# A new lead-in, logits in groups of eighty and a new order, in a kernel of windowed attention and a GELU layer

One core of a Trainium2 chip. The metric is the device time of one execution in microseconds (us), median over executions; a lower one is better.

## The reference

The input is normalised once and goes through two branches, whose results are added to it.

```python
xn = layernorm(x)                          # x: 2048 x 640, bf16
qkv = xn @ wqkv                            # 32 heads of 20
# query s sees keys s, s-2, ..., s-14 (8 of them); keys before the start are masked
attn = softmax(mask(q . k[s - 2w]) * 20**-0.5)
A = (sum_w attn[w] * v[s - 2w]) @ wo
B = gelu_tanh(xn @ w1 + b1) @ w2 + b2      # 640 -> 1536 -> 640
return x + A + B
```

## The kernel before

It works in four chunks of 512 positions (0 to 3), each of four blocks of 128. A planner in the kernel lists the pieces of work (name, engine, estimated duration, what they need), simulates the engines, and issues the pieces in the order in which they started in that simulation. Each engine gets its instructions in this order; in the traces below they wait for one another in it (a root whose input was ready at 4.87 us started at 7.15, behind a sum that waited for its data). `PE` is TensorE, `VE` VectorE, `SE` ScalarE, `DQ` the SyncE queue.

```python
# loads of the lead-in (cut)
nc.sync.dma_start(x_sb[:, 0, :], x_nb[:, 0, :])
nc.scalar.dma_start(x_sb[:, 1, :], x_nb[:, 1, :])
for s in range(3):                                     # q's, k's, v's weights, 800 KB each
    nc.sync.dma_start(wqkv[s][:], wqkv_v[:, :, s * D : (s + 1) * D])
    if s == 1:
        nc.sync.dma_start(x_sb[:, 2:BPC, :], x_nb[:, 2:BPC, :])
...
# 44 warm-up matmuls on zeros, then the plan
for _ in range(WARM):
    nc.tensor.matmul(idle[:, 0, :], lhsT=zeros[:], rhs=zeros[:], start=True, stop=True)
for t in make_plan(fns).run():
    t["fn"]()
```

For each block of chunk 0 VectorE takes the statistics (`st`), ScalarE the root (`rs`), VectorE the reciprocal and the normalised block (`rc`, `xn`), TensorE the transposes (`tp`), ScalarE copies them out of PSUM (`tc`), and TensorE projects block by block (`gj`, 128 columns a matmul, into the PSUM tile `gps`).

```python
def do_tp(n, bl, a, b):
    xn = tiles["xn", n, bl]
    tp = get(("tp", n, bl), lambda: psA.tile([P, 2 * CH], BF16, tag="acc", name="tp"))
    for t in range(a, b):
        nc.tensor.transpose(tp[:, t * P : (t + 1) * P], xn[:, t * P : (t + 1) * P], ident[:])
...
# logits: VectorE's eight products of q and shifted k fill four buffers "prod" (the whole pool);
# TensorE sums them by head: 20 matmuls for each buffer
group = 2 if n else 4
if wp % group == group - 1:
    wps = range(wp - group + 1, wp + 1)
    ...
    pl.add(f"lg{n}{wp}", PE, 0.16 + 0.52 * group, n - 1000, need, f("lg", n, wps), every + [L], slack=0.8)
...
def do_xs(n):                  # attention weights spread over each head's channels, half of it
    expand(nc.scalar, n, (2, 3))
def do_xd(n):                  # the other half
    expand(nc.sync, n, (0, 1))
```

ScalarE also empties the four PSUM accumulators of later chunks' projections (`pc`), applies GELU, and copies the output blocks.

## Time and profile before

| | before |
|---|---|
| time, median (range) | 215.03 us (215.01 to 215.15, 3 runs) |
| span of the profiled run | 212.4 us |
| TensorE, VectorE, ScalarE busy | 97%, 82%, 52% of the span |
| first useful matmul, last matmul (starts) | 7.03 us, 209.42 us |

The span goes from the first to the last instruction in the trace. The lines behind this table are shown and read in the prediction.

### The profile page before, as it was taken

To read this page: it belongs to the slowest core of one execution; us is meant where nothing else is said; L and a number is where in the kernel's file an instruction comes from. 1 tells how busy PE (TensorE), PEld (TensorE's weight loads), DVE (VectorE), ACT (ScalarE), POOL (GpSimd) and SP (SyncE) were. 2 spreads that over 40 slices of the span, in tenths; PEclk is the share of its full clock that TensorE was granted. 3 is DMA by queue.
4 is the path that set the end of the run, shared out by engine and by line. 5 is a ranking of instruction groups with operands and counts; after the bars stand their busy time and mean duration, and the time that the engine had idled before them with its cause. 6 is when DMAs were issued, how large, how long until landed. Compare 5 with 4: busy or idle time off the path is not lost.

```text
span 212.4 us, 3961 instructions
## 1 busy us (share of the span) xinstructions
PE 206.9 (97%) x1670; PEld 121.7 (57%) x1693; DVE 174.4 (82%) x178; ACT 109.5 (52%) x193; POOL 19.7 (9%) x37
## 2 busy tenths in 40 slices
PE   8999999999999999999999999999999999999994
PEld 8799845655545555555555555455555455555552
DVE  3579999759999997599996999999999999972001
ACT  3568997798574654931353883503752511341120
POOL 2000000000020024101100010101110011101130
PEclk9999999999999999999999999999999999999999
DMA  6999528916829199993120027202114611122214
GB/s 216 365 362 376 93 50 275 322 24 132 206 64 163 37 287 196 197 195 89 15 30 0 0 31 200 31 3 31 14 21 48 180 19 22 27 29 31 34 16 76
DMA packets 23465, 23.95 MB, mean 113 GB/s; under 512 B 9112, under 2 KB 20632, under 8 KB 23448
## 3 DMA queue, kind: packets, MB, share of 16 engines
q1 hardware_dynamic: 17864, 16.49, 28.3%
q0 software_dynamic: 4144, 4.92, 17.2%
q10 hardware_dynamic: 1440, 2.29, 3.9%
q8 instruction: 13, 0.21, 0.4%
q14 instruction: 4, 0.03, 0.1%
HBM read 10.00 MB, written 7.54 MB: 83 GB/s over the span
## 4 chain that ended last, share of the span: by engine, by line
PE 97%; issue 1%; DVE 0%; ACT 0%
PE lo L684 27%; PE hps L653 24%; PE pps L484 23%; PE gps L501 8%; PE hi L686 8%; PE L L557 4%; PE idle L725 2%; PE tp L437 1%; ACT xnT L441 0%; DVE osb L714 0%; DVE zeros L361 0%
## 5 line engine op out<-in xcount | busy, mean ns | idle before, releaser
L653 PE MATMUL hps<-xnT,w_sb 128*128 128x512 bf16 x235 | 54.1, 379 | 0.3
L684 PE MATMUL lo<-w_sb,hT 128*128 128x512 bf16 x183 | 51.8, 379 | 0.0
L631 DVE TENSOR_TENSOR pv<-vT,ax 128x2560 bf16<-128x2560 bf16 x32 | 45.9, 1484 | 1.7 <-PE L L557 1.7
L535 DVE TENSOR_TENSOR prod<-qT,kT 128x2560 bf16<-128x2560 bf16 x32 | 45.4, 1484 | 0.0
L686 PE MATMUL hi<-w_sb,hT 128*128 128x128 bf16 x192 | 40.3, 219 | 0.6 <-issue 0.2
L664 ACT ACTIVATE hT<-hps,b1T 128x512 bf16<-128x512 f32 x48 | 31.6, 687 | 17.0 <-PE hps L653 13.3
L653 PEld LDWEIGHTS <-w_sb 128*128 128x128 bf16 x240 | 23.0, 98 | 26.7
L640 DVE TENSOR_TENSOR pv<-pv 128x5120 bf16<-128x5120 bf16 x12 | 33.9, 2825 | 0.4
L684 PEld LDWEIGHTS <-hT 128*128 128x128 bf16 x192 | 18.7, 98 | 22.8 <-issue 0.6
L691 ACT CAST osb<-lo 128x512 bf16<-128x512 f32 x15 | 8.8, 585 | 44.0 <-issue 28.0
L697 POOL DMA_DIRECT2D out_dram<-osb x15 | 12.9, 863 | 110.5 <-ACT osb L692 110.5
L684 PE MATMUL lo<-wo,oT 128*128 128x512 bf16 x79 | 23.0, 379 | 0.0
L686 PEld LDWEIGHTS <-hT 128*128 128x128 bf16 x192 | 18.4, 98 | 1.5
L398 DVE BATCH_NORM_STATS2 stats<-x_sb 128x6 f32<-128x320 bf16 x32 | 14.0, 469 | 5.1 <-DMA x_sb<-in_A_x_dram 5.1
L484 PE MATMUL pps<-xnT,wq_sb 128*128 128x512 bf16 x71 | 16.9, 380 | 0.2
L484 PE MATMUL pps<-xnT,wv_sb 128*128 128x512 bf16 x73 | 16.9, 379 | 0.1
L686 PE MATMUL hi<-wo,oT 128*128 128x128 bf16 x80 | 16.9, 219 | 0.1
L484 PE MATMUL pps<-xnT,wk_sb 128*128 128x512 bf16 x73 | 16.8, 379 | 0.1
L705 DVE TENSOR_TENSOR osb<-lo,x_sb 128x512 bf16<-128x512 f32 x1 | 0.7, 692 | 16.1 <-PE lo L684 16.1
L520 ACT CAST qT<-pps 128x512 bf16<-128x512 f32 x15 | 8.8, 585 | 9.2 <-PE pps L484 9.2
L684 PEld LDWEIGHTS <-oT 128*128 128x128 bf16 x80 | 7.8, 98 | 9.4
L484 PEld LDWEIGHTS <-wk_sb 128*128 128x128 bf16 x75 | 8.7, 118 | 7.3 <-issue 0.2
(62 smaller groups left out, 205.9 us busy)
## 6 DMA issues: line engine op xcount, KB each, us to landing
w_sb<-in_B_w_dram SPq DMA_DIRECT2D x2, 1920.0 KB, 9.2
out_dram<-osb POOLq DMA_DIRECT2D x15, 160.0 KB, 3.4
ax<-attn SPq DMA_DIRECT2D x8, 256.0 KB, 5.4
ax<-attn ACTq DMA_DIRECT2D x8, 256.0 KB, 5.6
out_dram<-x_sb SPq DMA_DIRECT2D x3, 640.0 KB, 4.3
out_dram<-b2bc POOLq DMA_DIRECT2D x3, 640.0 KB, 8.2
x_sb<-in_A_x_dram SPq DMA_DIRECT2D x1, 1280.0 KB, 13.3
wq_sb<-in_A_wqkv_dram SPq DMA_DIRECT2D x1, 800.0 KB, 4.8
```

Of the source, the lines that this page charges most:

```text
L398: nc.vector.bn_stats(stats[:, i, :], x_sb[:, b, i * (D // 2) : (i + 1) * (D // 2)])
L484: nc.tensor.matmul(ps[:], lhsT=wqkv_p[which][:, ti, to, :], rhs=xnT[:, ti, :], start=(ti == 0), stop=(ti == KT - 1),)
L501: nc.tensor.matmul(ps[:, i, :], lhsT=wqkv_p[which][:, ti, to, :], rhs=tiles["xnT", 0][:, ti, cs], start=(ti == 0 and (i == 0 or b == KT an ...
L520: nc.scalar.copy(dest[:, to, off : off + CH], tiles["pps", n, which, to][:])
L535: nc.vector.tensor_tensor(out=prod[:, i, :, :], in0=qkv_tile(n, 0)[:], in1=qkv_tile(n, 1)[:, :, off : off + CH], op=ALU.mult,)
L631: nc.vector.tensor_tensor(out=pv[:, i, :, :].rearrange("p t (j c) -> p t j c", j=BPC), in0=qkv_tile(n, 2)[:, :, off : off + CH].rearrange( ...
L640: nc.vector.tensor_tensor(out=ta[:], in0=ta[:], in1=tb[:], op=ALU.add)
L653: nc.tensor.matmul(ps[:], lhsT=w1_sb[:, ti, ft * P : (ft + 1) * P], rhs=tiles["xnT", n][:, ti, :], start=(ti == 0), stop=(ti == KT - 1),)
L664: nc.scalar.activation(hT[:], tiles["hps", n, ft][:], ACT.Gelu_apprx_tanh, bias=b1T[:, ft : ft + 1], scale=1.0)
L684: nc.tensor.matmul(lo[:], lhsT=lhs, rhs=rhs[:, 0:CH], start=first, stop=last)
L686: nc.tensor.matmul(hi[:, 0 : D - CH], lhsT=lhs, rhs=rhs[:, CH:D], start=first, stop=last)
L697: nc.gpsimd.dma_start(rows, tiles["osb", n, bl][:], accum_op=ALU.add)
```

## The change

Its intent, as read from the diff: to start useful work earlier by having q's weights on the way first, to take block 1's statistics on an engine that is idle at that time (a sum, then a sum of squares on ScalarE), to copy block 0's and 1's transposes on two engines at once, to project later blocks in pairs (256 columns a matmul), to spend less on groups of logits, and to bring w1 earlier so that TensorE always has something to do. The planner gets new landing times and ranks. The diff, cut to its core:

```diff
+    for b in range(2):
+        nc.scalar.dma_start(x_sb[:, b, :], x_nb[:, b, :])
+    load_w(0)
+    load_x(2, BPC)
+    load_w(1)
+    load_w(2)
     ...
-            land = (4.0, 4.0, 9.6, 9.6)[bl] if n == 0 else (0.0, 13.3, 17.1, 17.1)[n]
+            land = (3.1, 3.6, 6.6, 6.6)[bl] if n == 0 else (0.0, 12.9, 21.8, 21.8)[n]
+            if n == 0 and bl == 1:
+                pl.add("sm", SE, 0.72, -99, [], f("sum1"), after=land)
+                pl.add("nm", SE, 0.22, -99, ["sm"], f("neg1"))
+                pl.add("me", VE, 0.12, -98, ["sm"], f("mean1"))
+                pl.add("sq", SE, 0.93, -99, ["nm"], f("sq1"))
+                pl.add("rs01", SE, 0.3, -99, ["sq"], f("sqrt", 0, 1, 2), table="sqrt")
+                pl.add("rc01", VE, 0.16, -99, ["rs01", "me"], f("rstd", 0, 1, 2))
+                continue
     ...
+                for u, a, b, eng, own in (("a", 0, 2, VE, "lo"), ("b", 2, KT, SE, "hi")):   # block 0: a PSUM tile each
     ...
-            group = 2 if n else 4
+        need = [f"qk{n}{x}{i}" for x in range(W // 2) for i in range(2)]
+        for wp in range(W // 2):          # all four buffers' logits follow one another
+            us, slack = (0.5, 0.0) if wp else (0.74, 0.8)
+            need = [pl.add(f"lg{n}{wp}", PE, us, n - 1000, need, f("lg", n, wp), [("prod", "qk", n, wp), L], slack=slack)]
-        pl.add(f"xs{n}", SE, 1.2, n - 1000, [f"at{n}"], f("xs", n), [at, ax])
+        pl.add(f"xs{n}", SE, 1.6, n - 1000, [f"at{n}"], f("xs", n), [at, ax])
     ...
+            nc.tensor.matmul(idle[:, 0, :], lhsT=ones, rhs=ones, start=True, stop=True)
```

Also in it: the maximum is subtracted in place in PSUM, w1 comes in two halves ahead of chunks 2 and 3, and the planner knows GpSimd's output writes as a queue.

## The prediction

> **What bounds the kernel now.** I read the page's busy shares and its chain first, to see which engine sets the end, then the list of what TensorE waits for, then the timeline of the lead-in, and last the timelines around one group of logits and around the last output of VectorE.
>
> ```profile
> PE 206.9 (97%) x1670; PEld 121.7 (57%) x1693; DVE 174.4 (82%) x178; ACT 109.5 (52%) x193; POOL 19.7 (9%) x37
> ...
> PE 97%; issue 1%; DVE 0%; ACT 0%
> ```
>
> TensorE is busy 97% of the span and the chain that ended last is TensorE for 97% of it. No other engine is on it for as much as a per cent. The waits of TensorE, summed over the whole span, are three:
>
> ```profile
> PE idle L725 <- DVE zeros L361: 1.0, 1, 1.0
> PE gps L501 <- ACT xnT L441: 0.5, 1, 0.5
> PE hi L686 <- issue: 0.2, 1, 0.2
> ```
>
> So there is no large wait to remove. What can go is time before the first useful matmul, and time per matmul. The lead-in, in the timeline (start, duration, engine, operation):
>
> ```profile
> 0.99 4.87 PE L725 MATMUL idle<-zeros 128*128 128x128 bf16 x44 [0.99 <-DVE zeros L361]
> ...
> 3.71 0.89 DVE L398 BATCH_NORM_STATS2 stats<-x_sb 128x6 f32<-128x320 bf16 x2 [2.77 <-DMA x_sb<-in_A_x_dram]
> ...
> 4.87 0.30 ACT L404 ACTIVATE std<-mv,eps_t 128x1 f32<-128x1 f32 x1 [2.18 <-DVE mv L400]
> 5.20 0.16 DVE L408 RECIPROCAL rstd<-std 128x1 f32<-128x1 f32 x1
> 5.40 0.63 DVE L424 TENSOR_SCALAR xn<-x_sb,mv,rstd 128x256 bf16<-128x256 bf16 x2
> ...
> 5.80 0.77 PE L437 MATMUL tp<-ident,xn 128*128 128x128 bf16 x5
> ...
> 6.61 0.75 ACT L441 COPY xnT<-tp 128x256 bf16<-128x256 bf16 x2 [1.44 <-PE tp L437]
> 7.03 1.28 PE L501 MATMUL gps<-xnT,wq_sb 128*128 128x128 bf16 x20 [0.46 <-ACT xnT L441]
> ```
>
> The reader is to see that useful work starts at 7.03 us and that its chain is block 0 of x: landing at 3.71, statistics, root, reciprocal, normalise, transpose, copy. The copy starts at 6.61 only after all five transposes, though its first part needs two. The last matmul starts at 209.42 (the closing five `hi` start at 209.20, 56 ns apart), so 202.4 us lie between the first and the last useful matmul and 3.0 us after it.
>
> A group of forty logits, and a group of eighty (chunk 0):
>
> ```profile
> 54.48 1.03 PE L484 MATMUL pps<-xnT,wv_sb 128*128 128x512 bf16 x4
> ...
> 55.44 1.27 PE L557 MATMUL L<-prod,head_of 128*32 128x256 bf16 x40
> ...
> 56.65 1.06 PE L484 MATMUL pps<-xnT,wv_sb 128*128 128x512 bf16 x3
> ```
>
> ```profile
> 36.83 2.37 PE L557 MATMUL L<-prod,head_of 128*32 128x256 bf16 x80
> 39.13 1.06 PE L484 MATMUL pps<-xnT,wq_sb 128*128 128x512 bf16 x3
> ```
>
> Forty take 55.44 to 56.65 = 1.21 us, eighty take 2.30 us: 27 ns each and 0.12 us per group. Before a group, four matmuls of 216 ns from 54.48 should end at 55.34, so about 0.09 us is lost on entering, and about 0.03 on leaving. One group's fixed price is thus about 0.24 us.
>
> [...] the row of 20 above gives (1.28 - 0.22)/19 = 56 ns, the row of 4 gives (1.03 - 0.38)/3 = 217. No row of before has N = 256 with full weights[...]. [...] The 44 warm-up matmuls are 0.107 us apart ((4.87 - 0.29)/43) and the first useful ones 0.056, so here the change fell between about 6.3 and 7.0 us[...]. [...] the trace has 0.93 for the two-pointer normalisation. [...] the page's GB/s row shows 362 to 376 in the first slices, so loads in the lead-in share a full pipe and only their order can be chosen.
>
> **The change part by part.**
> 1. *Start of useful work.* Block 0 now leaves from the ScalarE queue (where block 1 took 3.1 us from its issue at 0.75, against 2.9 for block 0 on the other), so it lands no earlier, about 3.7; q's weights leave first on the other queue, 0.46 earlier than now, so with 4.8 us to landing about 5.5, before they are wanted. Then 3.71 + 0.89 + 0.04 + 0.21 = 4.85, root 0.30 and reciprocal 0.16 with gaps to 5.37, first two slices normalised by 5.67, two transposes with their drain by 6.1, a 256-column copy of 0.36 now on VectorE and in its own PSUM tile by 6.45. First useful matmul about 6.5: **0.5 us** saved, nearly all of it from the copy no longer waiting for the other three transposes. The warm-up needs no VectorE memset and starts 0.2 earlier, ending at about 5.5; it doesn't limit.
> 2. *Projections of chunk 0.* Now 300 matmuls of N = 128: 300 x 0.056 = 16.8 us. After: 50 x 0.056 + 125 x 0.109 = 2.8 + 13.6 = 16.4. **0.4 us**, all of it on the path, since TensorE runs without gaps there. The two breaks for transposes (0.15 at 8.3 us, smaller later) may lose **0.1** more.
> 3. *Logits.* Chunks 1 to 3 go from six groups to three: 3 x 0.24 = **0.7 us** of TensorE.
> 4. *Block 1's statistics on ScalarE.* About 0.72 + 0.22 + 0.9 + 0.3 us of ScalarE, beside other work; VectorE loses 1.1 us. Not on the path, unless the first sum (block 1's landing, about 3.9 to 4.1, + 0.72 = 4.6 to 4.8) delays block 0's root at 4.87. That is tight, up to 0.2 us.
> 5. *In-place subtraction in PSUM, earlier w1, added DMA ordering in the plan.* They move no TensorE work. Earlier w1 only gives TensorE something else to do from some 16 us on; there is hardly a hole there to fill.
> The 737 matmuls of N = 512, the 272 of N = 128 in the outputs, and the 3.0 us after the last remain.
>
> Sum: start 6.5; work 202.4 - 0.4 - 0.1 - 0.7 = 201.2; end 3.0; span 210.7. For new small holes I add 0.3: 211.0. The measured time lies 215.03 - 212.4 = 2.6 above the span, so **213.6 us**, 0.7% less.
>
> **The rivals.**
> *VectorE takes the place.* A group of eighty holds all four product buffers until it is done, so VectorE can start no product of the earlier chunk for some 3 us in each of three chunks, where now half the buffers come back early. VectorE is nearly full from 23 us to 193:
>
> ```profile
> 131.11 11.30 DVE L535 TENSOR_TENSOR prod<-qT,kT 128x2560 bf16<-128x2560 bf16 x8
> 142.33 4.29 DVE L631 TENSOR_TENSOR pv<-vT,ax 128x2560 bf16<-128x2560 bf16 x3
> 146.53 1.22 DVE L570 TENSOR_REDUCE m<-L 128x128 f32<-128x1024 f32 x1
> ...
> 191.21 1.49 DVE L646 TENSOR_TENSOR oT<-pv 128x2560 bf16<-128x2560 bf16 x1 [1.58 <-PE hi L686]
> ```
>
> Here the three products at 142.33 run while the second half of the logits is computed; after the change they can't. Its last oT is done at 192.7 and first read at 195.89, and it waited 1.58 us for its buffer: some 4 to 5 us of slack. Against up to 9 us lost stand the new order, which can put later statistics (8 blocks, about 1 us each) into these gaps, and an earlier start of the first products by about 1 us. If VectorE comes out late by more than the slack, TensorE has only a few output blocks to do without oT: 1 to 4 us lost, a time of 214.5 to 217.
> *A long start.* If the clock is released a microsecond later than the first useful matmul, or block 0's root waits for ScalarE, part 1 gives back up to 0.5: 214.1.
> *No gain in part 1.* If block 0 shares the pipe with q's weights and lands at 4.2 instead of 3.7, the same: 214.1.
> *More than expected.* If q's weights and block 0 both come early (3.2 and 5.2), the start is 6.0 and the time 213.0. A gain over 2% would need 4.3 us, and the matmuls that remain leave no room for it.
>
> **Range and chances.** The sum is known to some 0.4 us on the fast side. On the slow side the open thing is the holes of the new order: none to two or three microseconds. Range 212.6 to 215.4. Faster by over 2%: 1%. Within 2%: 96%. Slower by over 2% needs over 4 us of new holes: 3%.
>
> **What would show it.** Right: first useful matmul at 6.2 to 6.7 us in the timeline; first copy of block 0 by VectorE directly behind two transposes; 256-column matmuls 0.109 apart; four groups of eighty in the chain; TensorE waits after the start below 0.5 us in sum; last `hi` matmul about 3.0 before the end. Wrong: TensorE waiting for VectorE or ScalarE in the list of waits, above all output matmuls on oT near the end; VectorE's last oT later than some 195 us; TensorE's busy time not lower by about 1 us; a start at or after 7.0.

## The result

| | before | after |
|---|---|---|
| time, median (range) | 215.06 us (215.01 to 215.15, 4 runs) | 220.33 us (219.17 to 220.58, 4 runs) |
| ratio, 95% interval | | 1.0234, 1.0209 to 1.0259 |
| span of the profiled run | 212.4 | 218.2 |
| first useful matmul, last matmul (starts) | 7.03, 209.42 | 8.84, 214.79 |

The change made the kernel slower by 2.3%. The mean granted clock of a run counts the time before the first entry of its clock record as full: the profiled run of the changed kernel lists 1.000, although TensorE is at half clock until 13.4 us (below). Two of its other three runs list 0.984, which is what 6.8 us at half clock after an earlier release would give (6.8/2/218 = 0.016). Ratios here are the mean time of one kernel's fast runs over that of the other's of the same rounds, so not quite the ratio of the medians quoted.

The page of the changed kernel, its busy shares and its chain:

```profile
PE 209.6 (96%) x1568; PEld 124.0 (57%) x1568; DVE 173.9 (80%) x177; ACT 108.2 (50%) x189; POOL 19.7 (9%) x37
...
PE 76%; DVE 16%; DMA 2%; ACTq 2%; ACT 1%; issue 1%
```

TensorE is still busy for nearly all of it, and its busy time is longer, although it has less to do: at half clock the matmuls take longer (fifteen in the lead-in below are 0.105 us apart, against 0.056 at full clock). The chain is no longer TensorE's alone. It begins with a DMA of x and ScalarE's queue. The waits of TensorE, in sum, number and longest:

```profile
PE tp L498 <- DVE xn L483: 2.4, 1, 2.4
PE pps L542 <- ACT vT L601: 1.8, 1, 1.8
PE idle L805 <- PEq L822: 0.8, 1, 0.8
PE pps L542 <- ACT kT L601: 0.3, 1, 0.3
```

The first is new, and stands before the first transpose. The lead-in in the timeline:

```profile
0.75 0.92 ACTq L384 DMA_DIRECT2D x_sb<-in_A_x_dram  x2
...
0.78 4.85 PE L805 MATMUL idle<-const-bfloat16-1.0 128*128 128x128 bf16 x44 [0.78 <-PEq L822]
...
4.66 0.21 DVE L444 BATCH_NORM_AGGREGATE mv<-stats 128x2 f32<-128x12 f32 x1
...
6.42 0.74 ACT L450 ACTIVATE xn<-x_sb 128x640 bf16<-128x640 bf16 x1 [3.22 <-DMA x_sb<-in_A_x_dram]
...
7.15 0.28 ACT L463 ACTIVATE std<-mv,eps_t 128x1 f32<-128x1 f32 x1
...
8.06 0.79 PE L498 MATMUL tp<-ident,xn 128*128 128x128 bf16 x5 [2.43 <-DVE xn L483]
...
8.49 0.29 DVE L503 COPY xnT<-tp 128x256 bf16<-128x256 bf16 x1 [0.20 <-PE tp L498]
...
8.84 1.76 PE L555 MATMUL gps<-xnT,wq_sb 128*128 128x128 bf16 x15
```

Block 0's statistics are done at 4.87. Its root starts at 7.15, because block 1's sum stands before it on ScalarE and waits until 6.42 for block 1. In the trace's DMA packets, ScalarE's queue moves block 0's share until about 3.3 us, nothing from there to 5.1, and block 1's share from 5.1 to 5.9; between the two SyncE's queue moves q's weights at 190 KB per half microsecond. TensorE stands from the end of its warm-up at 5.6 until 8.06, and then works at half clock: fifteen matmuls take (1.76 - 0.29)/14 = 0.105 us each. The trace's clock record has the release at 13.4 us, against 6.4 in the kernel before.

Later, the second wait of the list (timeline of 118 to 130 us):

```profile
117.35 7.09 DVE L710 TENSOR_TENSOR pv<-vT,ax 128x2560 bf16<-128x2560 bf16 x5
...
121.40 4.48 PE L542 MATMUL pps<-xnT,wv_sb 128*128 128x512 bf16 x20
...
124.47 2.38 ACTq L694 DMA_DIRECT2D ax<-attn  x2
...
126.89 0.25 ACT L608 COPY vT<-vT 128x70 bf16<-128x70 bf16 x1 [4.55 <-issue]
127.05 2.53 ACT L601 CAST vT<-pps 128x512 bf16<-128x512 f32 x5
...
127.68 1.24 PE L542 MATMUL pps<-xnT,wv_sb 128*128 128x512 bf16 x5 [1.80 <-ACT vT L601]
```

TensorE fills four accumulators with v's projections (20 matmuls) by 125.7. ScalarE can't empty them: the next thing in its order is to issue two transfers of attention weights, which wait until VectorE has read the tile of the chunk before (124.44), and then take 2.38 us to issue, where the plan counts 1.6.

The difference in span of 5.80 us, by the starts of the matmuls in the two traces:

| | before | after | difference |
|---|---|---|---|
| first useful matmul | 7.03 | 8.84 | +1.81 |
| matmuls and transposes at half clock after it (extra time) | 0 | 2.15 | +2.15 |
| the holes at 85.8, 125.5 and 175.3 us | 0 | 0.49 + 1.97 + 0.20 | +2.66 |
| all other time between first and last matmul | 202.39 | 201.14 | -1.25 |
| from the last matmul's start to the end | 2.99 | 3.42 | +0.43 |

The second row counts the 43 steps from 8.84 to the release at 13.4: they took 4.54 us, against 43 x 0.0557 = 2.39 at full clock.

### The profile page after: what moved, and what is told of

Read it like the earlier page. It is cut to its first block, busy times and chain, and to the rows that moved or that the text cites.

```text
span 218.2 us, 3727 instructions
## 1 busy us (share of the span) xinstructions
PE 209.6 (96%) x1568; PEld 124.0 (57%) x1568; DVE 173.9 (80%) x177; ACT 108.2 (50%) x189; POOL 19.7 (9%) x37
## 3 DMA queue, kind: packets, MB, share of 16 engines
q10 hardware_dynamic: 1584, 2.46, 4.4%
HBM read 10.00 MB, written 7.54 MB: 80 GB/s over the span
## 4 chain that ended last, share of the span: by engine, by line
PE 76%; DVE 16%; DMA 2%; ACTq 2%; ACT 1%; issue 1%
PE lo L763 22%; PE hps L732 22%; PE pps L542 15%; DVE pv L710 10%; PE gps L586 6%; PE hi L765 6%; PE L L637 3%; DMA x_sb<-in_A_x_dram 2%; PE gps L555 2%; ACTq L694 2%; DVE L L656 1%; DVE attn L684 1%; DVE m L650 1%; DVE rs L679 1%; PE tp L498 1%; DVE sums L674 1%
## 5 line engine op out<-in xcount | busy, mean ns | idle before, releaser
L763 PE MATMUL lo<-w_sb,hT 128*128 128x512 bf16 x192 | 53.4, 379 | 0.0
L442 DVE BATCH_NORM_STATS2 stats<-x_sb 128x6 f32<-128x320 bf16 x30 | 12.8, 466 | 3.7 <-DMA x_sb<-in_A_x_dram 3.7
L523 POOL DMA_DIRECT2D out_dram<-b2bc x4 | 5.3, 1322 | 102.6 <-DMA out_dram<-x_sb 102.4
L542 PEld LDWEIGHTS <-wv_sb 128*128 128x128 bf16 x75 | 8.7, 117 | 9.8 <-issue 2.7
```

The costliest lines, as they stand in the source:

```text
L442: nc.vector.bn_stats(stats[:, i, :], x_sb[:, b, i * (D // 2) : (i + 1) * (D // 2)])
L542: nc.tensor.matmul(ps[:], lhsT=wqkv_p[which][:, ti, to, :], rhs=xnT[:, ti, :], start=(ti == 0), stop=(ti == KT - 1),)
L763: nc.tensor.matmul(lo[:], lhsT=lhs, rhs=rhs[:, 0:CH], start=first, stop=last)
```

## The experiments

The theory after reading the traces: (a) block 1's transfer, whose packets start at 5.1 us, comes behind q's weights because they were issued ahead of it, although on the other queue; (b) ScalarE's order passes this on to block 0, whose root waits from 4.87 to 7.15; (c) the gap in TensorE's work, 5.6 to 8.06, costs the clock; (d) ScalarE's transfers in the middle cost another 2 us. The rivals are named with each run. In the experiments on the changed kernel, the planner's order is kept, and pieces are moved in the finished list only.

**Block 0's root ahead of block 1's sum.** On ScalarE alone.

```diff
+        order = make_plan(fns).run()
+        names = [t["name"] for t in order]
+        late = order.pop(names.index("sm"))
+        order.insert(names.index("rs00"), late)
```

> The changed kernel with one order on ScalarE altered: block 0's root is issued ahead of block 1's sum. Theory (ScalarE takes its instructions strictly in order, and block 1's sum, waiting for a block that lands at 6.4 us, holds up a root whose input was ready at 4.87): the root starts at about 4.9, the first useful matmul at about 6.5 instead of 8.84, the warm-up runs into it without a gap and the clock is released by about 7; time 216 to 217.5 instead of 220.3. Block 1 still lands at 6.4, so a new hole of 1 to 2 us stands before block 1's matmuls. Rival (the first matmul waits for q's weights, which land at about 5.9, or for the first copy): the start moves by less than 1 us and the time stays over 219.

Measured: 219.36 us (219.25 to 219.69), ratio to before 1.0212 (1.0192 to 1.0233). The expectation failed, and its timeline says why:

```profile
4.83 0.29 ACT L463 ACTIVATE std<-mv,eps_t 128x1 f32<-128x1 f32 x1 [1.65 <-DVE mv L444]
6.24 0.74 ACT L450 ACTIVATE xn<-x_sb 128x640 bf16<-128x640 bf16 x1 [1.12 <-DMA x_sb<-in_A_x_dram]
...
7.10 0.15 DVE L456 TENSOR_SCALAR mv<-acc 128x1 f32<-128x1 f32 x1 [2.38 <-ACT xn L450]
7.17 0.15 DVE L467 RECIPROCAL rstd<-std 128x1 f32<-128x1 f32 x1
```

The root is now early, at 4.83, but block 0's reciprocal comes at 7.17 all the same: on VectorE block 1's mean stands before it. The wait on one engine had a twin on another. First useful matmul: 8.54. The rival's figures came true (moved by less than 1 us, over 219), but not its reason, q's weights or the first copy.

**Block 1 ahead of q's weights, on SyncE's queue.**

```diff
-    for b in range(2):
-        nc.scalar.dma_start(x_sb[:, b, :], x_nb[:, b, :])
+    nc.scalar.dma_start(x_sb[:, 0, :], x_nb[:, 0, :])
+    load_x(1, 2)
     load_w(0)
```

> The changed kernel with block 1 issued on the SyncE queue ahead of q's weights (block 0 stays on ScalarE's). Theory (block 1's transfer stands behind q's 800 KB in the order of issue): block 1 lands at 3.8 to 4.1, the sum ends at about 4.9, the root starts by 5.0, first useful matmul at 6.4 to 6.7, clock released by about 7, no hole before block 1's matmuls: 215 to 216.5. The late waits of TensorE behind ScalarE (1.8 and 0.3 us) stay. Rival (block 1's lateness comes from ScalarE's queue itself, or q's weights now come too late): first matmul after 7.2 and the time over 218.

Measured: 216.53 us (216.39 to 217.29), ratio 1.0085 (1.0060 to 1.0111), of the same rounds as the run above. Block 1's sum starts at 3.57, the root at 5.02, and the clock record has the release at 4.9 us, kept to the end.

```profile
6.83 1.03 PE L555 MATMUL gps<-xnT,wq_sb 128*128 128x128 bf16 x15 [0.24 <-DMA wq_sb<-in_A_wqkv_dram]
```

The matmuls are 0.056 apart again ((1.03 - 0.22)/14 = 0.058, with one small break). One load moved, and most of the loss is back: 3.8 us by the medians, 3.2 by the two ratios (1.0234 and 1.0085 of 215). The price is that q's weights now end the wait for the first matmul. The late waits of 1.8 and 0.3 us on ScalarE are there as before, so they don't come of the late start.

**A longer warm-up.** `WARM = 72` in place of 44.

> The changed kernel with 72 warm-up matmuls instead of 44, nothing else. Theory (the 2.4 us without matmuls between the end of the warm-up at 5.6 and the first transpose at 8.06 let the clock go back, so that the projections run at 0.107 us a matmul until 13.4): the longer warm-up bridges the gap, the first useful matmul stays at about 8.8 but runs at 0.056 us, 2 to 2.5 us are saved: about 218. Rival (the late release comes from the ones as operands[...]): the projections are again at 0.107 us until 11 to 13.5, and the time is 220 or more.

Measured: 218.38 us (218.23 to 218.55), ratio 1.0164 (1.0145 to 1.0184). As expected:

```profile
8.59 1.00 PE L555 MATMUL gps<-xnT,wq_sb 128*128 128x128 bf16 x15
```

The start is still late, at 8.59, but the matmuls are at full clock, (1.00 - 0.22)/14 = 0.056. The release came at 4.6 us and the clock was kept. So of the lead-in's loss 1.5 us (by the ratios) to 2 us (by the medians) are the clock, and ones as operands are not to blame. The release does not come at the same time in every run of one lead-in: none came during the 44 matmuls of the changed kernel in its profiled run, and one came at 4.13 us in the run that follows here, which has the same lead-in, only to go back at 7.54, in the gap. In both TensorE came late to full clock, at 13.4 and 14.4. What sets the time of the release is not shown.

**All transfers of attention weights on SyncE's queue.**

```diff
-        expand(nc.scalar, n, (2, 3))
+        expand(nc.sync, n, (2, 3))
```

> The changed kernel with all four expansions of the attention weights issued on the SyncE queue, none on ScalarE's. Theory (ScalarE stands 4.5 us at 122 to 127 us waiting for the expanded tile's buffer and issuing two transfers of 2.4 us, while four accumulators wait to be emptied and TensorE stands 1.8 us): the waits of TensorE on ScalarE's copies (1.8 and 0.3 us) go, 1.5 to 2.3 us saved, about 218.3. Rival (VectorE or the DMA limits there, or the expanded tile comes later through one queue): the wait moves to VectorE, later matmuls wait for oT, saving under 0.7.

Measured: 218.99 us (218.25 to 219.26), ratio 1.0181 (1.0152 to 1.0210). Both waits on ScalarE's copies are gone (2.1 us by the list of waits), but a new one has come, of TensorE on VectorE:

```profile
PE lo L763 <- DVE oT L725: 0.8, 1, 0.8
```

So theory and rival were each partly right: 1.1 us (by the ratios) to 1.3 us (by the medians) are gained, and behind ScalarE stood VectorE, which finished the second chunk's `oT` only just after TensorE came for it. The clock record of this run shows a loss in the lead-in's gap: release at 4.13, half clock from 7.54, release again at 14.37.

**Everything of block 0 before anything of block 1's sums, on both engines.** The loads stay as changed.

```diff
+        late = [t for t in order if t["name"] in ("sm", "nm", "sq", "rs01", "me")]
+        # taken out, and put back in this order behind block 0's second copy, "tc00b"
```

> The changed kernel with its loads as they are, and the order on both engines altered: everything of block 0 up to its second copy is issued before anything of block 1's sums, on ScalarE and (the mean) on VectorE. The earlier order run moved ScalarE's part alone, and the wait reappeared on VectorE, where block 1's mean stood before block 0's reciprocal. Theory (in-order issue on both engines holds block 0 back, nothing else): root at 4.85, first useful matmul at 6.4 to 6.6, a new hole of about 1.5 to 2 us before block 1's matmuls, whose sum starts at about 6.3; clock released by about 7 and kept; time 217 to 218. Rival (block 0 waits for q's weights or something else): first matmul after 7.5, time over 218.5.

Measured: 220.20 us (218.64 to 220.34), ratio 1.0221 (1.0185 to 1.0257): no better than the changed kernel. In the profiled run, which was the quick one, the first useful matmul starts at 6.20, earlier than in any other run here, so order alone did hold block 0 back. But block 1 now comes later still (its transposes at 9.66), and TensorE stands 2.5 us in between. This run kept its clock (mean granted clock 1.000). The three others show 0.992, which is what 3.41 us at half clock in 218 would give (3.41/2/218 = 0.008); in the run with block 0's root ahead, which also lists 0.992, the clock record has it at half from 7.72 to 11.14.

```profile
6.20 1.00 PE L555 MATMUL gps<-xnT,wq_sb 128*128 128x128 bf16 x15
9.66 0.45 PE L498 MATMUL tp<-ident,xn 128*128 128x128 bf16 x5 [2.46 <-DVE xn L483]
```

The late block 1 costs its time in either place: with the clock kept, this run took 218.64, and the run with the longer warm-up 218.38. In most runs the gap seems to cost the clock as well; that is read from their mean clock, since they have no trace.

**The new first loads in the kernel before.** Nothing else changed there.

```diff
-    nc.sync.dma_start(x_sb[:, 0, :], x_nb[:, 0, :])
+    nc.scalar.dma_start(x_sb[:, 0, :], x_nb[:, 0, :])
     nc.scalar.dma_start(x_sb[:, 1, :], x_nb[:, 1, :])
```

> The kernel before with its first loads alone in the new order: blocks 0 and 1 both on ScalarE's queue, q's weights first on SyncE's. Everything else as before. Theory ([...] block 1, issued third, comes behind q's 800 KB; statistics in strict order then hold up block 0): block 1 lands at 6.0 to 6.5 us instead of about 3.8, the first half of its statistics, issued before block 0's reciprocal, holds block 0 until about 6.7, first useful matmul at 8.2 to 8.6, the clock may go back: 217 to 219 against 215.0. Rival (only the new ScalarE statistics are at fault): under 216.

Measured: 217.67 us (217.16 to 218.78), ratio 1.0127 (1.0092 to 1.0162). In the profiled run block 1 landed at 7.46, a microsecond later than expected, and the first useful matmul came at 9.71, at half clock (four in 0.59 us, about 0.10 apart).

```profile
7.46 0.49 DVE L398 BATCH_NORM_STATS2 stats<-x_sb 128x6 f32<-128x320 bf16 x1 [1.88 <-DMA x_sb<-in_A_x_dram]
7.87 0.15 DVE L408 RECIPROCAL rstd<-std 128x1 f32<-128x1 f32 x1
```

Moving one 160 KB load to the other queue, which puts q's weights ahead of block 1, costs the kernel before 2.6 us by itself. Block 0 landed later too, at 4.46 instead of 3.71, which is some 0.7 us of it; the rest is block 0's reciprocal standing behind the first half of block 1's statistics, as the two lines show. The new statistics are not needed for the harm.

One rival has no run of its own. Wherever block 1 came late, it was also the second transfer on ScalarE's queue, and wherever it came early it was the first on its queue. The packets speak for q's weights: in the five traces of the changed loads block 1's first packet started when 743 to 760 of q's 800 KB had been moved, at 4.9 to 5.1 us, although ScalarE's queue had had nothing to move since about 3. In this run it started at 5.6, after all of q's weights and some 130 KB of k's, whose load was issued just after it.

**The two edits together**, block 1's load and the transfers of attention weights.

> The changed kernel with block 1 on SyncE's queue ahead of q's weights, and all expansions on SyncE's queue: the two single edits together. Theory (the lead-in's loss of 3.8 and the late wait's 1.3 are independent): 216.5 - 1.3 = 215.2, within 0.4; TensorE's waits on ScalarE's copies gone, a wait of about 0.9 us on oT near 133 us. Rival (the hole at 136 us of the expansion run came of the cold start): no wait on oT, 214.3.

Measured: 215.50 us (215.21 to 216.22), ratio 1.0024 (1.0003 to 1.0046). The two gains add up (216.5 - 1.3 = 215.2 was expected). The wait on `oT` stays at 0.8 us, so it is not a consequence of the cold start.

**The same with the logits in groups of forty again** in chunks 1 to 3.

```diff
+        for n in range(1, NCH):
+            ready = max([by[f"qk{n}{x}{i}"]["end"] for x in (0, 1) for i in (0, 1)] + [by[f"ex{n - 1}"]["end"]]) + 1.5
+            early = [by[f"lg{n}0"], by[f"lg{n}1"]]
+            # these two put in front of the first piece planned to start after "ready"
```

> The same two edits, and in chunks 1 to 3 the logits again in two groups of forty: the first group is issued as soon as its products are planned to be ready plus 1.5 us, all else in the same order. By the prediction's part 3 each group has a fixed price of 0.24 us on TensorE: 3 x 0.24 = 0.7 us slower than the run with the two edits, about 215.9. Rival (groups of eighty cost VectorE its buffers, 2 us in each chunk, and that costs more): equal or faster, as products of the earlier chunk can start before the last forty; then the wait on oT is shorter too.

Measured, in the same rounds: 214.99 us (214.77 to 215.34), ratio to before 0.9997 (0.9980 to 1.0015). The interval excludes the 0.7 us loss that part 3 of the prediction implies. The rival, equal or faster, held; that it is faster is not certain, since this interval and that of the run before it overlap. The wait on `oT` is gone. What forty to a group gives VectorE is seen after the last product of chunk 1 (VectorE's timeline, first with eighty, then with forty):

```profile
58.61 1.48 DVE L616 TENSOR_TENSOR prod<-qT,kT 128x2560 bf16<-128x2560 bf16 x1
62.30 2.89 DVE L710 TENSOR_TENSOR pv<-vT,ax 128x2560 bf16<-128x2560 bf16 x2 [2.21 <-PE L L637]
```

```profile
58.63 1.49 DVE L616 TENSOR_TENSOR prod<-qT,kT 128x2560 bf16<-128x2560 bf16 x1
60.03 2.89 DVE L710 TENSOR_TENSOR pv<-vT,ax 128x2560 bf16<-128x2560 bf16 x2
```

With eighty, VectorE stands 2.2 us until the logits give the product buffers back. With forty it goes on at once, and loses 1.3 us later, at the maximum.

**The end.** In the run above, with one more reordering: the first two pieces of the last output block go behind the other blocks, as in the kernel before.

> The run with both edits and groups of forty (215.0), and the first two pieces of the last output block moved behind the other blocks, as in the kernel before. Theory (the last accumulating write of a block is issued 2.1 to 2.3 us before the last matmul ends, against 3.6 before, takes 0.9 to issue and 3.4 to land, and so ends the program: 4.0 us from the last matmul's start to the end against 3.0): the write is issued 1.3 us earlier relative to the end, the end comes 3.0 to 3.2 after the last matmul, 0.7 to 0.9 us saved: 214.2. Rival (the end is set by the last small write or by closing work): no change, 215.0.

Measured: 216.43 us (215.73 to 217.65), ratio 1.0061 (1.0016 to 1.0106). The theory fell. The last accumulating write is issued earlier, yet the end still comes 3.99 us after the last matmul's start. The reordering itself added a wait of TensorE on the copy of an output block (0.7), and in the profiled run q's weights landed later (a wait of 1.0 against 0.2). SyncE's instructions at the end show another part of the tail. It waits for the DMA semaphores one after another, in nine instructions about 0.06 us apart. In the changed kernel the last write's semaphore is met in the second, at 216.88, and the others are gone through after it until 217.38. In the kernel before it is in the last. That makes the 0.43 us by which the changed kernel's tail is longer. The run here, at 3.99, has 0.5 us more between two later instructions of SyncE (213.11 and 213.59); what for stays open.

**The first copy, in the kernel before.** Block 0's two groups of transposes get a PSUM tile each, and nothing else changes.

```diff
-        tp = get(("tp", n, bl), lambda: psA.tile([P, 2 * CH], BF16, tag="acc", name="tp"))
+        pool, tag = (psA, "acc") if bl else (psO, "hi" if a else "lo")
+        tp = get(("tp", n, bl, a), lambda: pool.tile([P, 2 * CH], BF16, tag=tag, name="tp"))
```

> The kernel before with one thing from the new lead-in: block 0's two groups of transposes write a PSUM tile each, so the first copy needs not wait for the last three transposes. Loads, statistics and order as before. Prediction's part 1 by itself: first copy at about 6.15 instead of 6.61, first useful matmul at 6.6 instead of 7.03, about 0.4 us less: 214.6. Rival (the clock[...] takes it back, or the second copy holds the third slice's matmuls): 215.0.

Measured, over five rounds: 214.94 us (214.50 to 215.23), ratio 0.9987 (0.9951 to 1.0024), no difference that is clear; the 0.5 us of the prediction (a ratio of 0.998) is not excluded either. Two of the eleven runs of the kernel before in these rounds were at 216.3 and 217.5 with a clock of 0.992, which widens the interval. The first copy came at 6.05 and the first useful matmul at 6.47, 0.56 earlier, as the prediction had it. In the trace the time was given back by two new waits:

```profile
PE tp L438 <- DVE xn L424: 0.7, 1, 0.7
PE gps L502 <- DMA wk_sb<-in_A_wqkv_dram: 0.4, 1, 0.4
```

TensorE, earlier by half a microsecond, now waits for k's weights and later for a normalised block. In this trace loads and VectorE set the pace behind the first matmul, and starting ahead of them won nothing.

**A version meant to beat both**: the two edits, forty to a group, block 1's transposes copied at once by ScalarE, and w1 in one load (one transfer fewer, which turns the order of the closing waits).

> A version meant to beat both: block 1 ahead of q's weights, expansions on SyncE's queue, forty logits to a group, and two more things. Block 1's transposes are copied by one ScalarE copy (split over two engines they read one PSUM tile and ran one after the other: 8.17 to 8.97). And w1 comes in one load, one transfer fewer, so that the last two writes get the last of SyncE's closing waits: in the changed kernel SyncE waited for the last write first of eight and went through the other seven after it, 0.06 each. Theory: last matmul's start to the end 3.0 to 3.5 us instead of 3.4 to 4.0, hole near 8.5 us shorter by 0.1 to 0.3; 214.0 to 214.5 against 215.0 for before. Rival (the end is not set by the order of those waits; w1 in one load comes too late): 215 or more.

Measured, over five rounds: 214.91 us (214.56 to 216.53, 7 runs), ratio 0.9978 (0.9942 to 1.0015). That is level with before and not shown to be faster. The closing part did shorten, to 3.0 us after the last matmul's start with the last writes last in SyncE's waits, so the order of those waits counts, as far as one profile shows. The profiled run was the slowest of the seven (216.53): q's weights landed at 7.5 us there and w1 1.4 us after TensorE wanted it. Whether w1 in one load has that price in the other runs is not shown.

## Why the prediction was wrong

It forecast 213.6 us (212.6 to 215.4) and 96% for a difference within 2%; the time is 220.33, slower by 2.3%.

- **Part 4 is the step that failed.** It has "block 1's landing, about 3.9 to 4.1", takes from this that the sum might delay block 0's root by "up to 0.2 us", and calls all else beside other work. That fits block 1's 3.1 us in the kernel before, where it had been issued ahead of q's weights. In the changed kernel it was issued behind them, and landed at 6.42. The root was delayed by 2.3 us. The durations that part 4 gives block 1's pieces on ScalarE, 0.72, 0.22, 0.9 and 0.3, are close to the planner's in the diff; the trace has 0.74, 0.19, 0.83 and 0.29, and 0.19 for reading out each of the two sums. Part 1's own chain was right up to there (block 0's statistics done at 4.87 against 4.85), and the first copy did follow directly behind two transposes (0.29 us on VectorE, where 0.36 was estimated). The first useful matmul came at 8.84 instead of 6.5. Moving block 1's load (216.5 us) and making the same move in the kernel before (217.7) show that the new order of the loads is the cause; the two order runs show that moving the sum alone doesn't help while the block is late.
- **The rival "a long start" had the right mechanism and a wrong size.** It allowed 0.5 us for the clock. It did not see that a delay of the root also makes a gap after the warm-up, and that TensorE then comes late to full clock, at 13.4 us against 6.4. This took 2.15 us of extra time in the profiled run, and the run with 72 warm-up matmuls, with its release at 4.6, got 1.5 to 2 back.
- **"For new small holes I add 0.3"** was 2.66. The prediction looked for them behind VectorE; 2.46 of it were behind ScalarE, whose transfers stand in order with the copies that empty TensorE's accumulators. A wait for ScalarE was among the signs of being wrong, but no line of the prediction asked how ScalarE's own queue fills. A comparable transfer took 1.3 to 2.4 us to issue in the kernel before, where TensorE had other work.
- **The rival "VectorE takes the place"** is true in kind, at less than its 1 to 4 us, and was hidden by the holes before it. Once those were gone, TensorE waited 0.8 us for `oT`, and the median with groups of forty was 0.5 us lower than with groups of eighty. Part 3's price per group was right (0.09 before, 0.11 in it, 0.01 to 0.03 after), but in this order TensorE's saving of 0.7 us did not show in the time, beside VectorE's 2.2 us without a buffer.
- **Right:** the work that remains for TensorE. 201.2 us were predicted between first and last matmul, and 201.14 remain after half clock and holes are taken off. The 256-column matmuls are 0.109 us apart, as estimated (a straight line through before's 0.056 at 128 columns and 0.216 at 512 gives the same).
- **Smaller misses.** The end took 3.4 us instead of 3.0 (order of the closing waits). The time lies 2.1 us above the span of the same run (220.26 and 218.2), not 2.6, which had set the median of before against the span of a quick run. And part 1, tested alone, brought its 0.56 us at the start and no clear gain at the end, so that a start at 6.5 would be worth 0.5 us is not shown.

## What to carry to other kernels

When loads change places, work out anew what is issued ahead of each: block 1 stayed on its queue, and its landing time, which belonged to its old place, did not hold (6.42 us against an expected 3.9 to 4.1). Where engines work in order, one late input should be behind everything that doesn't need it, on every engine that touches it; moving it on one engine moved the wait to the next (root at 4.83, reciprocal still at 7.17). And the gap in TensorE's first microseconds cost twice here, once as a gap (a wait of 2.4 us) and once as clock (1.5 to 2 us), so a warm-up should last until the first useful matmul can really start.

## What the traces showed of loads and clock

- Block 1 (160 KB, ScalarE's queue), issued after q's weights (800 KB, SyncE's queue), did not share with them in the changed kernel: its packets moved from 5.1 to 5.9 us, the first when 757 KB of q's had been started, and it landed at 6.42 instead of about 3.6 when issued ahead. The order of issue was not kept strictly everywhere: with the same loads in the kernel before, block 1's packets began at 5.6, after some 130 KB of k's weights.
- In the run with block 0's root ahead, the clock was released at 4.31, went back at 7.72 and came again at 11.14, with TensorE idle from 5.09 to 7.77. With the attention weights on SyncE's queue it was released at 4.13, went back at 7.54 and came again at 14.37, with TensorE idle from 5.0 to 8.14. With everything of block 0 first, it was released at 4.84 and kept over a gap of 2.5 us that ended at 9.66. What makes the difference is not shown.
- In the profiled run of the changed kernel 4.8 us of warm-up matmuls back to back (0.8 to 5.6 us) released nothing; the clock came at 13.4. The same warm-up had it at 4.31 and 4.13 in the first two runs named above. In the kernel before, with 44 matmuls from 0.99 on, it came at 6.4, and with the new first loads at 3.69. No fixed time from the first matmul to the release can be read from this.
- Two transfers of 256 KB in the middle of the kernel before held ScalarE for 1.3 to 2.4 us.
